# K and Q split two heads at a time, and put in place by DMA

## The chip, the cores and the metric

One core of a Trainium2 chip runs the whole program as one launch. The metric is device time in microseconds. A core has TensorE (PE in the profile; its weight loads are PEld), VectorE (DVE), ScalarE (ACT), GpSimd (POOL) and SyncE (SP), which here only issues DMAs. Each engine works through its own instructions in the order in which they were written; semaphores order the engines among each other.

## The reference

Inputs q, k, v are (2, 8, 576, 64): batch B, heads H, positions S, head width D. The output of an attention goes through two mixture-of-experts layers:

```python
scores = scale * np.matmul(q, k.transpose(0, 1, 3, 2))        # scale = 1/8
x = (np.log1p(np.abs(rel)) / psi_i)[..., None]                # rel = i - j
bias = np.maximum(x @ w1 + b1, 0.0) @ w2                      # (S, S, H)
scores = scores + bias.transpose(2, 0, 1)[None]
attn = softmax(scores)                                        # max taken off, then exp
x = (attn @ v), heads side by side: (1152, 512)
# layer 1: logits = normalised x @ normalised expert_emb / tau; layer 2: logits = x @ w_gate
# each: best expert per token, out = gate * relu(x @ w1[e]) @ w2[e]
```

All in float32, 8 experts, w1[e] (512, 1024), w2[e] (1024, 512).

## The kernel before

A float32 value is carried as two fp32r parts, a high one (a cast) and a low one (the rest), so that products keep their accuracy. **Attention** runs over 9 tiles `t` of 128 query rows; tiles 0, 2, 4, 6 belong to batch 0, tiles 1, 3, 5, 7 to batch 1, and tile 8 takes the last 64 rows of both. A tile has 8 heads: 72 steps (`heads`). For a step, `s_mm` (L317) multiplies Q by K on PE (4 matmuls, twice 288 columns, with the two parts of Q as weights), `s_max` (L325, DVE) adds the bias and finds the maximum, `s_exp` (L335, ACT) takes the exponent, `p_turn` (L349) transposes on PE, `p_out` (L359, L362, ACT) and `p_lo` (L368, DVE) copy out, and `av` (L388) multiplies by V on PE. `s_mm` and `s_max` of a step are written three steps ahead (`LEAD`), `s_exp` one.

**K** is resident: `K[p, head, j]` holds, for each of 16 (batch, head) pairs, the high part of all 64 dimensions in partitions 0 to 63 and the low part in partitions 64 to 127. So that both halves can be made in place, k is loaded twice, into both halves of `kraw` (L160). `k_split` (L162) casts all 128 partitions on ACT (L165) and overwrites the lower part on DVE (L166), for 2 heads at a time (`KCH`), 8 times in all. **Q** of a tile is `Q[p, part, head, i]` with the same 64 dimensions in both halves of the partitions; it is loaded twice (L143) and split on ACT (L151) and DVE (L152; for tile 0 on POOL).

**The bias** of 128 query rows is built in 18 pieces (`pc`) of 32 keys: `bias_mask` (L247, DVE), `bias_mm` (L260, 16 matmuls on PE), and `bias_out`, which either goes by ACT (L272) and POOL (L273, L274) or, where it is `direct`, by two DVE instructions (L268, L269). The first 18 pieces are made ahead of the first step (here called the preparation, together with splitting V); the pieces of later rows are spread over the steps by the table `sched`. `DIRECT` lists the direct pieces of the preparation. `KSLOT` says behind which step which K chunk is split, beside chunks 0 and 1 in the preparation.

`moe_setup2` (L637) prepares the router of the first layer: `g.en`, the scaled embeddings of the experts, and `g.wg`, the split gate weights of the second. The **experts** (from some 235 us on) then stream 64 weight chunks for each layer.

What is written in this order is handed to a scheduler, which orders the instructions of each engine by its own estimates; the order on an engine is therefore not that of the code, and moves when any part of the code does. Each DMA signals one of 8 semaphores in turn, and a DMA waits until the one 8 places ahead of it has landed.

Of the kernel before, what the change touches and what calls it, by code (L numbers as in the profile page):

```python
# [54 lines left out]
def layouts(inp):  # L55

    q, k, v = inp["q"], inp["k"], inp["v"]
    w1, b1, w2 = inp["w1"], inp["b1"], inp["w2"]
    qt = q.transpose(0, 3, 1, 2)
    vb = v.reshape(BH // 2, 2, S, D)  # L60
    vm = np.stack([vb[:, 0, 0:512], vb[:, 1, 64:576]], 1).reshape(BH, 4, P, D)
    vr = np.concatenate([vb[:, 0, 512:576], vb[:, 1, 0:64]], 1)
    wv = np.concatenate([w1.reshape(-1), b1.reshape(-1), w2.reshape(-1)])
    wc = np.concatenate([w1.reshape(HID, 1), b1.reshape(HID, 1), w2], 1)
    return {
        "a_q": np.stack([qt[:, :, :, i * P:(i + 1) * P] for i in range(4)]).reshape(4, B, D, H * P),
        "a_qt": qt[:, :, :, 512:576].reshape(B, D, H * 64),
        "a_k": k.transpose(0, 3, 1, 2).reshape(B, D, H * S),
        "a_v": vm.reshape(BH // 2, 2, 4, P, D).transpose(3, 1, 0, 2, 4).reshape(P, BH * 4 * D),
        "a_vr": vr.transpose(1, 0, 2).reshape(P, BH // 2 * D),  # L70
        "a_wv": wv.reshape(1, 320),
        "a_wc": np.concatenate([wc] * 4, 0),
    }
# [20 lines left out]
def attention(tc, ctx, g, a, out, setup, on_tile, on_slot):  # L94
# [38 lines left out]
    def q_load(t):  # L133
        o = tiles[t] = Ctx()
        o.e, o.av, o.Pt, o.pt, o.ps, o.qs = {}, {}, {}, {}, {}, []
        o.it = t // 2
        for b in ([t % 2] if t < 8 else [0, 1]):
            qr = soon.tile([P, H, P], F32, tag="qraw", name="qraw")
            if t == 8:
                nc.gpsimd.memset(qr, 0.0)  # L140
            for d in range(2):
                if t < 8:
                    nc.sync.dma_start(qr[d * 64:(d + 1) * 64].rearrange("p h i -> p (h i)"), a["a_q"][o.it, b])  # L143
                else:
                    nc.sync.dma_start(qr[d * 64:(d + 1) * 64, :, b * 64:b * 64 + 64], a["a_qt"][b].rearrange("d (h i) -> d h i", h=H))
            o.qs.append((b, qr, bw.tile([P, 2, H, P], F32R, tag="Q", name="Q", bufs=3)))
        o.sums = bw.tile([P, H], F32, tag="sums", name="sums")

    def q_split(t):
        for b, qr, Q in tiles[t].qs:  # L150
            nc.scalar.copy(Q[:, 0], qr)  # L151
            (nc.vector if t else nc.gpsimd).tensor_tensor(Q[:, 1], qr, Q[:, 0].bitcast(F32), ALU.subtract)  # L152

    kraws = {}

    def k_load(c):
        b, c4 = divmod(c, H // KCH)
        kr = kraws[c] = kp.tile([P, KCH * S], F32, tag="kraw", name="kraw")
        for d in range(2):
            nc.sync.dma_start(kr[d * 64:(d + 1) * 64], a["a_k"][b][:, c4 * KCH * S:(c4 + 1) * KCH * S])  # L160
# [12 lines left out]
    nc.vector.memset(zero, 0.0)
# [460 lines left out]
def moe_setup2(tc, g, a, pool, psum_tile):  # L634
    nc = tc.nc
    c = g.const
    g.trih = c.tile([P, P], F16, name="trih")  # L637
    nc.vector.tensor_copy(g.trih, g.tri)
    g.onesh = c.tile([P, P], F16, name="onesh")
    nc.vector.memset(g.onesh, 1.0)  # L640
    g.ioh = c.tile([P, P], F16, name="ioh")
    nc.vector.tensor_copy(g.ioh, g.iota)
    g.cap = c.tile([P, 1], F32, name="cap")
    nc.vector.tensor_copy(g.cap, g.cap64[:, 0:1])
    g.capp = c.tile([P, 1], F32, name="capp")
# [631 lines left out]
```

## Time and profile before

| | us |
|---|---|
| median of 3 runs | 635.23 (634.74 to 635.35) |
| the profiled execution | 635.61 |
| its span, first to last instruction | 633.7 |
| PE / DVE / ACT / POOL busy | 559.8 / 449.0 / 379.0 / 241.5 |
[...]

The span is read by stages: a share of busy time over the whole of it mixes the preparation, the steps of attention and the experts, and each has another engine that is full.

### The profile page before, as it was taken

How to read it: one execution, taken by the hardware profiler on the slowest of the kernel's cores; microseconds unless marked ns; L12 is line 12 of the kernel's file. 1: busy time of each engine (PE TensorE's matmuls, PEld its weight loads, DVE VectorE, ACT ScalarE, POOL GpSimd, SP SyncE). 2: the span in 40 equal slices, each digit the busy share in tenths (PEclk: the TensorE clock that was granted, in tenths of full speed). 3: DMA queues.
4: the chain of work that ended last, by engine and by line, in shares of the span. 5: the costliest groups of instructions: out<-in, count | busy, mean ns of one | idle time of the engine just before them, and what ended most of it. 6: DMA issues, size and time to landing. Idle time of an engine off the chain costs nothing. (4 is left out here: it accounts for less than half of the span.)

```text
span 633.7 us, 12729 instructions
## 1 busy us (share of the span) xinstructions
PE 559.8 (88%) x4770; PEld 477.5 (75%) x4770; DVE 449.0 (71%) x738; ACT 379.0 (60%) x629; POOL 241.5 (38%) x223
## 2 busy tenths in 40 slices
PE   2558889999999999799999999999879999899991
PEld 2447788998889997577788788777657887677771
DVE  6988999989987766889921541389668716738960
ACT  3347768877778755488723632587517536647840
POOL 3662643555545152324531312133232313424440
PEclk9568999999999999899999999999999999999996
DMA  7933651211000862789950451286938905847900
GB/s 215 324 90 79 166 179 36 69 53 43 19 19 26 206 234 84 241 272 342 359 169 25 137 186 49 76 279 213 348 89 234 350 35 169 271 145 228 327 5 8
DMA packets 48820, 101.42 MB, mean 160 GB/s; under 512 B 12820, under 2 KB 14740, under 8 KB 48448
## 3 DMA queue, kind: packets, MB, share of 16 engines
q1 hardware_dynamic: 41552, 92.12, 45.4%
q0 software_dynamic: 6272, 7.49, 3.6%
q8 instruction: 62, 1.02, 0.7%
q14 instruction: 54, 0.44, 0.2%
q10 hardware_dynamic: 880, 0.35, 0.2%
HBM read 97.47 MB, written 13.67 MB: 175 GB/s over the span
## 5 line engine op out<-in xcount | busy, mean ns | idle before, releaser
L911 DVE TENSOR_TENSOR wl<-raw,wh 128x1024 fp32r<-128x1024 f32 x125 | 156.2, 1289 | 19.5 <-ACT wh L898 15.9
L964 PE MATMUL py<-wh,hT 128*128 128x512 f32 x400 | 141.2, 404 | 0.0
L898 ACT CAST wh<-raw 128x1024 fp32r<-128x1024 f32 x110 | 113.9, 1050 | 5.1 <-ACTq L1169 2.6
L994 DVE TENSOR_TENSOR hT<-pt,hT 128x512 fp32r<-128x512 f32 x50 | 34.6, 692 | 92.4 <-ACT hT L993 92.4
L964 PEld LDWEIGHTS py<-wh,hT 128*128 128x128 f32 x400 | 75.2, 188 | 15.1
L260 PE MATMUL pm<-wmov,mask 128*128 128x64 f16 x1296 | 58.0, 203 | 29.6 <-DVE wmov L235 12.3
L273 POOL TENSOR_TENSOR btmp<-abst,xp 128x256 f32<-128x256 f32 x52 | 47.9, 920 | 84.0 <-ACT abst L272 81.9
L260 PEld LDWEIGHTS <-mask 128*128 128x128 f16 x1296 | 52.0, 105 | 36.3 <-DVE mask L247 25.3
L964 PE MATMUL py<-wl,hT 128*128 128x512 f32 x200 | 78.2, 391 | 0.0
L317 PE MATMUL s<-K,Q 128*128 128x288 f32 x320 | 64.0, 322 | 6.1 <-DVE mx L325 4.8
L335 ACT ACTIVATE P<-sb,mx 128x576 f32<-128x576 f32 x72 | 55.8, 776 | 17.5 <-DVE mx L325 15.4
L325 DVE CUSTOM_DVE_ANT_0 sb<-s,bias 128x576 f32<-128x576 f32 x72 | 53.4, 747 | 15.9 <-PE s L317 9.1
L247 DVE TENSOR_TENSOR mask<-toep,T 128x1024 f16<-128x1024 f16 x72 | 56.6, 792 | 1.5 <-PE pm L260 1.2
L964 PE MATMUL ph<-wh,xh 128*128 128x512 f32 x120 | 50.6, 421 | 7.8 <-PEq L1169 7.0
L349 PE MATMUL pt<-ident,P 128*128 128x128 f32 x324 | 53.1, 283 | 1.5 <-ACT pT L359 0.9
L317 PEld LDWEIGHTS s<-K,Q 128*128 128x128 f32 x320 | 46.9, 194 | 7.6 <-DVE mx L325 5.7
L272 ACT ACTIVATE abst<-pm,swi 128x512 f32<-128x512 f32 x52 | 35.7, 686 | 28.2 <-PE pm L260 28.0
L274 POOL TENSOR_TENSOR bias<-abst,btmp 128x256 f32<-128x256 f32 x52 | 50.0, 962 | 4.1
L993 ACT CAST hT<-pt 128x512 fp32r<-128x512 f32 x50 | 29.4, 587 | 36.4 <-PE pt L988 32.9
L964 PE MATMUL ph<-wh,xl 128*128 128x512 f32 x120 | 47.8, 398 | 1.4 <-issue 1.4
L964 PE MATMUL ph<-wl,xh 128*128 128x512 f32 x120 | 47.5, 396 | 0.0
L1033 POOL DMA_INDIRECT y_tok<-y,si x13 | 17.1, 1313 | 69.0 <-ACT y L1025 42.4
(218 smaller groups left out, 1144.9 us busy)
## 6 DMA issues: line engine op xcount, KB each, us to landing
raw<-m_w_dram SPq DMA_DIRECT2D x64, 512.0 KB, 5.2
raw<-n_w_dram SPq DMA_DIRECT2D x64, 512.0 KB, 5.1
kraw<-a_k_dram SPq DMA_DIRECT2D x16, 288.0 KB, 4.3
qraw<-a_q_dram SPq DMA_DIRECT2D x16, 256.0 KB, 4.2
out_dram<-zero SPq DMA_DIRECT2D x9, 256.0 KB, 7.3
y_tok<-zero SPq DMA_DIRECT2D x9, 256.0 KB, 4.8
x_tok<-x SPq DMA_DIRECT2D x8, 256.0 KB, 2.2
yt<-y_tok SPq DMA_DIRECT2D x4, 512.0 KB, 4.6
```

The costliest lines, as they stand in the source:

```text
L247: nc.vector.tensor_tensor(m, w, T[:, i0:i0 + P].unsqueeze(1).to_broadcast([P, 8, P]), ALU.is_gt)
L260: nc.tensor.matmul(pm[:, :, :, gq * 4:gq * 4 + 4], m[:, gq], wmov[:, part], start=part == 0, stop=part == 1)
L272: nc.scalar.mul(ab_, pm, isw)
L273: nc.gpsimd.tensor_tensor(tmp, ab_[:, 0], xp, ALU.mult)
L274: nc.gpsimd.tensor_tensor(biases[it][:, :, cs], ab_[:, 1], tmp, ALU.add)
L317: nc.tensor.matmul(ps[:, half, :288], Q[:, part, h], K[:, b * H + h, half * 288:half * 288 + 288], start=i == 0, stop=i == last)
L325: nc.vector.tensor_tensor_reduce(sb.rearrange("p (t j) -> p t j", t=2), o.ps.pop(h)[:, :, :288], biases[o.it][:, h].rearrange("p (t j) -> ...
L335: nc.scalar.activation(o.Pt[hp][:, x * S:(x + 1) * S], sb, AF.Exp, bias=mx, scale=-1.0, accum_out=o.sums[:, h:h + 1])
L349: nc.tensor.transpose(pt[:, cc], src, ident)
L898: eng.copy(hi, r)
L911: eng.tensor_tensor(lo, self.raw.pop((ge, j)), hi.bitcast(F32), ALU.subtract)
L964: self.nc.tensor.matmul(ps, x[a_][:, xs], w[b_][:, ws], start=first and i == 0, stop=last and i == 2)
```

## The change

K and Q are loaded once, with two heads above each other: head 2c in partitions 0 to 63, head 2c+1 in partitions 64 to 127. The split makes the high and the low part side by side in a scratch tile (`ks`, `qs`, one buffer each), and four DMAs from SBUF to SBUF put the parts where the matmuls want them. `Q` becomes `Q[p, head % 2, part, head // 2, i]`. The split of tile 8's Q and its POOL memset work on half the columns too. Of the preparation's bias pieces, 17 (the last) is direct in place of 15. K chunks 1 and 2 are written into the preparation's steps 8 and 14, the others two steps earlier than before. Two instructions of `moe_setup2` go from DVE to ACT.

```diff
-DIRECT = 1, 3, 5, 7, 9, 11, 13, 15
+DIRECT = 1, 3, 5, 7, 9, 11, 13, 17
-KSLOT = {0: 2, 2: 3, 4: 4, 6: 5, 8: 6, 10: 7}
+KSLOT = {0: 3, 2: 4, 4: 5, 6: 6, 8: 7}
...
-            for d in range(2):
-                if t < 8:
-                    nc.sync.dma_start(qr[d * 64:(d + 1) * 64].rearrange("p h i -> p (h i)"), a["a_q"][o.it, b])
...
+                nc.sync.dma_start(qr.rearrange("p h i -> p (h i)"), a["a_q"][o.it, b])
...
     def q_split(t):
         for b, qr, Q in tiles[t].qs:
-            nc.scalar.copy(Q[:, 0], qr)
-            (nc.vector if t else nc.gpsimd).tensor_tensor(Q[:, 1], qr, Q[:, 0].bitcast(F32), ALU.subtract)
+            qs = soon.tile([P, 2, H // 2, P], F32R, tag="qs", name="qs", bufs=1)
+            nc.scalar.copy(qs[:, 0], qr)
+            (nc.vector if t else nc.gpsimd).tensor_tensor(qs[:, 1], qr, qs[:, 0].bitcast(F32), ALU.subtract)
+            for half in range(2):
+                for par in range(2):
+                    nc.sync.dma_start(Q[half * 64:half * 64 + 64, par].bitcast(F32), qs[par * 64:par * 64 + 64].bitcast(F32))
...
     def k_split(c, eng):
         kr = kraws.pop(c)
-        dst = K[:, c * KCH:(c + 1) * KCH].rearrange("p h j -> p (h j)")
-        nc.scalar.copy(dst, kr)
-        eng.tensor_tensor(dst[64:], kr[64:], dst[64:].bitcast(F32), ALU.subtract)
-        if c + 2 < BH // KCH:
+        ks = soon.tile([P, 2, S], F32R, tag="ks", name="ks", bufs=1)
+        nc.scalar.copy(ks[:, 0], kr)
+        eng.tensor_tensor(ks[:, 1], kr, ks[:, 0].bitcast(F32), ALU.subtract)
+        for par in range(2):
+            for part in range(2):
+                nc.sync.dma_start(K[part * 64:part * 64 + 64, 2 * c + par].bitcast(F32), ks[par * 64:par * 64 + 64, part].bitcast(F32))
+        if c + 2 < BH // 2:
             k_load(c + 2)
...
-        if x == 12:
-            k_split(1, nc.vector)
+        if x in (8, 14):
+            k_split(x // 6, nc.vector)
...
-    nc.vector.tensor_scalar(g.en, g.en, ss, None, ALU.mult)
+    nc.scalar.mul(g.en, g.en, ss)
...
-    nc.vector.tensor_copy(g.wg[:, :, 0], g.wgr)
+    nc.scalar.copy(g.wg[:, :, 0], g.wgr)
```

Line numbers of the changed kernel are 1 to 5 higher (its K low part is L170, its Q low part L154, its copies L157 and L173, a mask L252, `s_max` L330).

On DVE, in the preparation behind the first mask of the bias (`mask`), before:

```order
L247 TENSOR_TENSOR mask<-toep,T 128x1024 x3
L654 TENSOR_SCALAR ess<-ess 8x1
L663 CAST wg<-wgr 128x4x8
L655 RECIPROCAL ess<-ess 8x1
L664 TENSOR_TENSOR wg<-wgr,wg 128x4x8
L656 TENSOR_SCALAR en<-en,ess 8x512
L268 SCALAR_TENSOR_TENSOR btmp<-pm,swi,xp 128x256
L247 TENSOR_TENSOR mask<-toep,T 128x1024
L166 TENSOR_TENSOR K<-kraw,K 64x1152
```

and at the same place of the changed kernel:

```order
L252 TENSOR_TENSOR mask<-toep,T 128x1024 x2
L170 TENSOR_TENSOR ks<-kraw,ks 128x576
L252 TENSOR_TENSOR mask<-toep,T 128x1024
L273 SCALAR_TENSOR_TENSOR btmp<-pm,swi,xp 128x256
L252 TENSOR_TENSOR mask<-toep,T 128x1024
```

The cast and the scaling have left DVE, and the small instructions of the router stand some 40 rows further down.

On DVE at the first four `s_max` (the rows named ISA), before; of the masks, 20 stand ahead of the first `s_max`, and both K chunks 0 and 1:

```order
L661 COPY enT<-pt 128x32
L247 TENSOR_TENSOR mask<-toep,T 128x1024
L325 ISA sb,mx<-s,bias 128x576
L325 ISA mx 128x1
L325 ISA sb,mx<-s,bias 128x576
L325 ISA mx 128x1
L247 TENSOR_TENSOR mask<-toep,T 128x1024
L325 ISA sb,mx<-s,bias 128x576
L325 ISA mx 128x1
L325 ISA sb,mx<-s,bias 128x576
```

and now, where 22 masks, K chunk 0 and the Q of tile 1 stand ahead of it, and K chunk 1 (`ks`) behind the first:

```order
L252 TENSOR_TENSOR mask<-toep,T 128x1024 x2
L154 TENSOR_TENSOR qs<-qraw,qs 128x512
L330 ISA sb,mx<-s,bias 128x576
L330 ISA mx 128x1
L252 TENSOR_TENSOR mask<-toep,T 128x1024
L170 TENSOR_TENSOR ks<-kraw,ks 128x576
L330 ISA sb,mx<-s,bias 128x576
L330 ISA mx 128x1
L273 SCALAR_TENSOR_TENSOR btmp<-pm,swi,xp 128x256
L274 SCALAR_TENSOR_TENSOR bias<-pm,swi,btmp 128x8x32
L252 TENSOR_TENSOR mask<-toep,T 128x1024
L373 SCALAR_TENSOR_TENSOR ptl<-pt,pth 128x512
```

The third `s_max` follows directly; it is the first that needs K chunk 1. On both sides, chunk c (from 2 on) is split one or no step ahead of its first use.

On SP, from the nine writes of zeros into the output on, the queue now reads:

```order
L200 DMA out_dram<-zero 128x512 x9
L157 DMA Q<-qs 64x1024 x4
L173 DMA K<-ks 64x576 x4
L163 DMA kraw<-a_k_dram 128x576
L130 DMA xp<-c_xpos_dram 128x576
L157 DMA Q<-qs 64x1024
L173 DMA K<-ks 64x576 x4
L163 DMA kraw<-a_k_dram 128x576
L157 DMA Q<-qs 64x1024
L173 DMA K<-ks 64x576 x4
```

Before, only loads and writes of zeros stood there; now 72 copies are in this queue (8 K chunks and 10 splits of Q, 4 each), and a matmul waits for each of them.

## Rows read from the trace of the kernel before

**Rows 1.** The page: busy time, share of the span and instructions of each engine.

```profile
PE 559.8 (88%) x4770; PEld 477.5 (75%) x4770; DVE 449.0 (71%) x738; ACT 379.0 (60%) x629; POOL 241.5 (38%) x223
```

**Rows 2.** By stretch: length; busy PE, PEld, DVE, ACT, POOL; clock, DMA, GB/s.

```profile
12.00:41.00 29.00, 16.52 (x266) 14.82 (x267) 27.94 (x56) 13.87 (x20) 18.51 (x17) 0.62 0.82 247
41.00:48.00 7.00, 4.16 (x61) 3.78 (x58) 3.99 (x8) 2.06 (x3) 6.61 (x7) 0.88 0.33 91
48.00:60.00 12.00, 9.76 (x95) 9.12 (x95) 10.58 (x21) 9.22 (x19) 1.38 (x2) 0.86 0.23 54
60.00:100.00 40.00, 33.78 (x510) 30.44 (x507) 38.24 (x69) 31.40 (x58) 22.81 (x24) 1.00 0.57 160
100.00:140.00 40.00, 39.74 (x594) 38.14 (x593) 37.91 (x80) 31.79 (x66) 18.51 (x22) 1.00 0.20 55
140.00:200.00 60.00, 55.49 (x834) 51.83 (x832) 54.44 (x112) 45.49 (x96) 34.45 (x38) 1.00 0.09 26
200.00:235.00 35.00, 35.00 (x395) 34.12 (x392) 23.57 (x58) 26.02 (x59) 13.22 (x9) 1.00 0.67 197
```

**Rows 3.** In order of time, DVE, ACT and POOL, 8 to 23 us: start, duration.

```profile
8.96 0.22 DVE L642 CAST ioh<-cm 128x128 f16<-128x128 f32 x1
...
12.40 1.90 DVE L247 TENSOR_TENSOR mask<-toep,T 128x1024 f16<-128x1024 f16 x3
...
14.68 1.15 ACT L165 CAST K<-kraw 128x1152 fp32r<-128x1152 f32 x1 [0.45 <-DMA kraw<-a_k_dram]
14.73 2.34 POOL L152 TENSOR_TENSOR Q<-qraw,Q 128x1024 fp32r<-128x1024 f32 x1
...
14.84 2.96 DVE L663 CAST wg<-wgr 128x32 fp32r<-128x32 f32 x1
...
17.95 0.94 DVE L656 TENSOR_SCALAR en<-en,ess 8x512 f32<-8x512 f32 x1
...
20.32 1.77 DVE L166 TENSOR_TENSOR K<-kraw,K 64x1152 fp32r<-64x1152 f32 x1
```

**Rows 4.** In order of time, DVE, up to the first `s_max`.

```profile
44.25 0.73 DVE L247 TENSOR_TENSOR mask<-toep,T 128x1024 f16<-128x1024 f16 x1
48.00 0.76 DVE L325 CUSTOM_DVE_ANT_0 sb<-s,bias 128x576 f32<-128x576 f32 x1 [3.01 <-POOL bias L274]
```

**Rows 5.** The low parts of K and Q by line: shortest, median, longest ns.

```profile
L166 DVE TENSOR_TENSOR K<-kraw,K x8: 1354/1355/1768, 20.3 to 87.1; 64x1152 fp32r<-64x1152 f32 x8
L152 DVE TENSOR_TENSOR Q<-qraw,Q x9: 1212/1221/1747, 56.0 to 206.1; 128x1024 fp32r<-128x1024 f32 x9
```

**Rows 6.** DVE by line: busy us, mean ns; and one `s_mm` on PE.

```profile
L247 DVE TENSOR_TENSOR mask<-toep,T 128x1024 f16<-128x1024 f16 x72 | 56.6, 792 | 1.5 <-PE pm L260 1.2
...
L368 DVE SCALAR_TENSOR_TENSOR ptl<-pt,pth 128x512 f16<-128x512 f32 x36 | 24.5, 679 | 4.7 <-ACT pth L362 4.5
...
L268 DVE SCALAR_TENSOR_TENSOR btmp<-pm,swi,xp 128x256 f32<-128x256 f32 x29 | 13.7, 473 | 2.5 <-PE pm L260 2.0 <-POOL bias L274 0.4
...
216.72 0.78 PE L317 MATMUL s<-K,Q 128*128 128x288 f32 x4
```

**Rows 7.** DMA issues: count, KB, us to landing; and L276, the first `bias<-bias`.

```profile
bias<-bias SPq DMA_DIRECT2D x3, 576.0 KB, 5.8
...
x_tok<-x SPq DMA_DIRECT2D x2, 128.0 KB, 2.3
...
DMA to landing us min/median/max: 4.6/4.6/4.6
```

**Rows 8.** SP's queue in order of time: start, time to issue.

```profile
18.26 8.53 SPq L195 DMA_DIRECT2D out_dram<-zero  x9
...
67.03 1.10 SPq L160 DMA_DIRECT2D kraw<-a_k_dram  x2
...
211.96 0.59 SPq L278 DMA_DIRECT2D bias<-bias  x1
213.59 0.32 SPq L679 DMA_DIRECT2D x_tok<-x  x1
```

More of the change, by code (lines that the diff above doesn't have):

```diff
@@ L28 @@
 EXPM = 0x7F800000
-KCH = 2
 PSC = 4096.0
-DIRECT = 1, 3, 5, 7, 9, 11, 13, 15
+DIRECT = 1, 3, 5, 7, 9, 11, 13, 17
 XSTEP = 1, 2, 3, 4
 WA = 0, 0, 4
-KSLOT = {0: 2, 2: 3, 4: 4, 6: 5, 8: 6, 10: 7}
+KSLOT = {0: 3, 2: 4, 4: 5, 6: 6, 8: 7}
 def consts():
@@ L58, in layouts, with pairs @@
     w1, b1, w2 = inp["w1"], inp["b1"], inp["w2"]
-    qt = q.transpose(0, 3, 1, 2)
+    def pairs(x):
+        return x.reshape(B, H // 2, 2, S, D).transpose(0, 2, 4, 1, 3).reshape(B, P, H // 2, S)
+    qt = pairs(q)
     vb = v.reshape(BH // 2, 2, S, D)
@@ L65, in layouts @@
     return {
-        "a_q": np.stack([qt[:, :, :, i * P:(i + 1) * P] for i in range(4)]).reshape(4, B, D, H * P),
-        "a_qt": qt[:, :, :, 512:576].reshape(B, D, H * 64),
-        "a_k": k.transpose(0, 3, 1, 2).reshape(B, D, H * S),
+        "a_q": np.stack([qt[:, :, :, i * P:(i + 1) * P] for i in range(4)]).reshape(4, B, P, H // 2 * P),
+        "a_qt": qt[:, :, :, 512:576].reshape(B, P, H // 2 * 64),
+        "a_k": pairs(k).transpose(0, 2, 1, 3),
         "a_v": vm.reshape(BH // 2, 2, 4, P, D).transpose(3, 1, 0, 2, 4).reshape(P, BH * 4 * D),
@@ L137, in q_load @@
         for b in ([t % 2] if t < 8 else [0, 1]):
-            qr = soon.tile([P, H, P], F32, tag="qraw", name="qraw")
+            qr = soon.tile([P, H // 2, P], F32, tag="qraw", name="qraw")
             if t == 8:
                 nc.gpsimd.memset(qr, 0.0)
-            for d in range(2):
-                if t < 8:
-                    nc.sync.dma_start(qr[d * 64:(d + 1) * 64].rearrange("p h i -> p (h i)"), a["a_q"][o.it, b])
-                else:
-                    nc.sync.dma_start(qr[d * 64:(d + 1) * 64, :, b * 64:b * 64 + 64], a["a_qt"][b].rearrange("d (h i) -> d h i", h=H))
-            o.qs.append((b, qr, bw.tile([P, 2, H, P], F32R, tag="Q", name="Q", bufs=3)))
+                nc.sync.dma_start(qr[:, :, b * 64:b * 64 + 64], a["a_qt"][b].rearrange("p (h i) -> p h i", h=H // 2))
+            else:
+                nc.sync.dma_start(qr.rearrange("p h i -> p (h i)"), a["a_q"][o.it, b])
+            o.qs.append((b, qr, bw.tile([P, 2, 2, H // 2, P], F32R, tag="Q", name="Q", bufs=3)))
         o.sums = bw.tile([P, H], F32, tag="sums", name="sums")
@@ L150, in q_split @@
         for b, qr, Q in tiles[t].qs:
-            nc.scalar.copy(Q[:, 0], qr)
-            (nc.vector if t else nc.gpsimd).tensor_tensor(Q[:, 1], qr, Q[:, 0].bitcast(F32), ALU.subtract)
+            qs = soon.tile([P, 2, H // 2, P], F32R, tag="qs", name="qs", bufs=1)
[4 more added lines that the diff above has]
+                    nc.sync.dma_start(Q[half * 64:half * 64 + 64, par].bitcast(F32), qs[par * 64:par * 64 + 64].bitcast(F32))
     kraws = {}
     def k_load(c):
[L157 to L160, printed above, removed]
+        kr = kraws[c] = soon.tile([P, S], F32, tag="kraw", name="kraw")
+        nc.sync.dma_start(kr, a["a_k"][c // 4, c % 4])
     def k_split(c, eng):
         kr = kraws.pop(c)
-        dst = K[:, c * KCH:(c + 1) * KCH].rearrange("p h j -> p (h j)")
-        nc.scalar.copy(dst, kr)
-        eng.tensor_tensor(dst[64:], kr[64:], dst[64:].bitcast(F32), ALU.subtract)
-        if c + 2 < BH // KCH:
+        ks = soon.tile([P, 2, S], F32R, tag="ks", name="ks", bufs=1)
[5 more added lines that the diff above has]
+        if c + 2 < BH // 2:
             k_load(c + 2)
-    kp = soon
     zero = soon.tile([P, DM], F32, name="zero", bufs=1)
@@ L316, in s_mm @@
                 for part in range(2):
-                    nc.tensor.matmul(ps[:, half, :288], Q[:, part, h], K[:, b * H + h, half * 288:half * 288 + 288],
+                    nc.tensor.matmul(ps[:, half, :288], Q[:, h % 2, part, h // 2], K[:, b * H + h, half * 288:half * 288 + 288],
                                      start=i == 0, stop=i == last)
```

## The prediction

> **What bounds the kernel now.** The page comes first, and it misleads: PE is busy for 88% and DVE for 71% of the span [rows 1], as if DVE hardly mattered. The table of stretches shows where that is wrong [rows 2]. From 12 to 41 us DVE is busy for 27.94 of 29 us and PE for 16.52: the preparation is DVE's. From 48 to 100 us DVE is busy for 48.8 of 52 us, PE for 43.5. From 100 to 140 both are nearly full (PE 39.74 of 40, DVE 37.91), to 200 neither quite, and from 200 to 235 PE has no gap at all. So an instruction taken off DVE is worth its length before 100 us, little from 100 to 200, and nothing from 200 to 235. The experts behind are not touched, and start when attention is done: what is won ahead of 235 us shifts them as a whole.
>
> In order of time the preparation shows what fills DVE [rows 3]: a cast of 128x32 that lasts 2.96 us, where another cast with four times the columns took 0.22; it begins just after POOL's pass over Q (14.73 to 17.07) and ends with it. Then 0.94 us for an 8x512 scaling, and 1.77 for K chunk 0. Further on, before the first `s_max` at 48.00, stands a wait of 3.01 us for POOL's last bias piece [rows 4].
>
> **The change, part by part.**
>
> *Low parts of K and Q.* DVE's time follows the columns: 1152 take 1.355 us and 1024 take 1.221 [rows 5]. Half the columns: 0.68 and 0.61 us, by those rates. ACT's casts halve too, but ACT has room (31.4 of 40 us [rows 2]), so they count nothing, as do the cast and the scaling that go to it. Loads halve. Only the first matters: DVE now comes to chunk 0 behind its third mask, at some 13.7 us, and ACT's cast of it waited for the load until 14.68 [rows 3]. With one load of Q ahead of it instead of two, and half the bytes, it should land by 13: 0 to 1.5 us, I take 0.
>
> *The preparation,* from the first `s_max` at 48.00 backwards. Off DVE: the wait 3.0 (piece 17 goes to DVE, POOL's last is now 16, and the order puts two masks and a Q split in the place of the wait), the cast 2.9, the scaling 0.9, of chunk 0 1.77 - 0.68 = 1.1, and chunk 1, which moves behind the first `s_max`, 1.4 [rows 5]: 9.3 us. On DVE: two masks that stood later, 1.4 at 0.7 each [rows 4], tile 1's Q split, 0.6, and POOL's Q pass, which with half the columns should take 1.2 us instead of 2.34, and now lies beside DVE's second and third mask. What that costs is open: nothing, as three masks ran at 0.63 us each (1.90 for three [rows 3]) beside POOL's instruction ahead of the pass, or 1.2, as the cast waited for the whole pass. I take 0.8, nearer the cast, since it is the same POOL instruction. Added 2.8, net 6.5: first `s_max` at 41.5.
>
> [...]
>
> The state at that `s_max` is not the old one: two masks (1.4) and a Q split (1.2 at its old length) are done, chunk 1 (0.68) is not. That is another 1.9 us that DVE needn't spend later.
>
> *48 to 100 us.* Chunks 2 to 7 save 6 x 0.68 = 4.1, tile 2's Q 0.6. DVE thus offers 6.5 + 1.9 + 4.7 = 13.1 us by the old 100 us mark.
>
> *The copies* take some of it back. For K the chain is: low part on DVE, SP issues the copy, it lands, `s_mm` (0.78 [rows 6]), `s_max`. No copy of 144 KB between 64 partitions is in the trace. The nearest row is 64 rows of x to HBM, 128 KB, 2.3 us to landing; the far end is the 576 KB copy of the bias inside SBUF, 4.6 us, as many bytes as all four K copies together [rows 7]. With 0.1 for the signal the need is 3.2 to 5.5 us. The second low copy is issued 0.55 later (two loads take 1.10 [rows 8]), so I take 3.5, near the row of like size.
>
> What covers it is what stands on DVE between the low part and the first `s_max` that needs the chunk, at 0.79 a mask, 0.47 a direct half, 0.68 a `p_lo`, 0.75 an `s_max` [rows 4, 6]: for chunks 1 to 7 3.2, 3.2, 4.0, 4.5, 3.8, 4.1 and, with two masks and a `p_lo` alone, 2.3 us. At a need of 3.5 DVE waits 0.3 + 0.3 + 1.2 = 1.8 us, at 3.2 some 0.9, at 5.5 some 13. K chunk 0 and tile 0's Q come behind the nine writes of zeros, which were issued by 26.8 us [rows 8]; eight copies at 0.55 and some 3 us to land bring them to 34, 6 us ahead of the first `s_mm`. Q splits of later tiles stand at least 4 steps, some 10 us, ahead of use, against 4 copies of 0.55 and some 3 us to land: nothing. Without that cover each would cost up to 5.
>
> [...]
>
> So DVE leaves 13.1 - 1.8 = 11.3. PE sets another limit: from 41 to 100 it is busy for 47.7 us [rows 2]. In the new order PE starts `s_mm` some 1.5 us ahead of the first `s_max`, at 40, with 2.2 us of later bias matmuls already done: 45.5 us of work. If it idles as from 60 to 100 us (15.5%), the mark falls at 40 + 53.8 = 93.8, 6.2 us early; if as from 100 to 140 (0.7%), 14 us early. With DVE's load lighter it lies between; I take the middle of 6.2 and 11.3: **8.8 us**.
>
> *100 to 235 us.* Seven Q splits save 4.3 us of DVE; PE has 4.8 us of idle time there, all before 200 [rows 2]. I take 1.0 of a possible 0 to 4.3. Against it, SP's order now puts the store of x ahead of the third copy of the bias of tile 8, which used to go first, 1.6 us apart, with two Q copies behind [rows 8]: 0 to 1.9 us on tile 8's first step, of which I take 0.5.
>
> **Sum:** 8.8 + 1.0 - 0.5 = 9.3 us off the profiled 635.61 is 626.3. The median of the runs lies 0.38 lower: **625.9**.
>
> **Rivals.**
> - *The copies land as late as the bias copy* (need 4.6 to 5.5): DVE waits 7 to 13 us at the K chunks, and the gain is 0 to 6. For it speaks that all four are in flight together; against it the 2.3 us of the x rows. Some 631.
> - *Slower:* the same place, but each K copy sits behind others in SP's queue. A Q copy of 256 KB stands directly ahead of six of the seven K groups from chunk 1 on. From a need of some 5.5 us on, the waits eat everything that DVE saves; at 6.5 they come to 20 us, and the time is 642. Against it: the Q copies there depend on splits that DVE has finished earlier.
> - *POOL stays the last:* pieces 14, 15, 16 now follow each other on it. If the first `s_max` waits for it as before, up to 2 us less: 628.
> - *PE is the bound after all,* with its old idle share: 6.2 - 1.8 + 0.5, 631. Or it follows DVE fully and the tiles to 200 us gain too: 620.
>
> **Chances.** The forecast with its spread, POOL included, 0.70; fuller gain, 0.08; late copies or PE's old share, gain still above 1.3 us (0.2%, about what a measurement of this kernel can tell), 0.10; nothing left, 0.05; slower by more than 0.2%, 0.07. Faster 0.88, same 0.05, slower 0.07. The range reaches from the fuller gain, 620, to the late copies, 632; it leaves out the far end of both.
>
> **What would show it.** [...] The prediction is wrong if `s_mm` waits for a K copy by over 2 us at every chunk, if POOL or the queue of SP holds the first `s_max`, or if PE's idle share to 100 us stays at 15%.

## The result, and the profile after

The change makes the kernel slower: 640.76 us median (639.07 to 642.45) against 635.29, ratio 1.0086, 95% interval 1.0062 to 1.0109. Measured a second time (run e8 below) it is 639.69 us, ratio 1.0029 [1.0000, 1.0058]. The loss is thus 0.3 to 0.9%, the smaller figure at the edge of what its interval tells, where a gain of 1.5% was forecast. The profiled execution took 639.07 us, with a span of 637.3.

The page of the changed kernel, busy times and instructions, answers to [rows 1]: DVE has 9.6 us less to do.

```profile
PE 564.9 (89%) x4770; PEld 481.2 (76%) x4770; DVE 439.4 (69%) x736; ACT 371.5 (58%) x631; POOL 237.0 (37%) x223
```

The stretches, with the columns of [rows 2]:

```profile
12.00:41.00 29.00, 17.09 (x300) 14.84 (x301) 26.96 (x59) 12.14 (x19) 21.23 (x20) 0.76 0.76 233
41.00:48.00 7.00, 4.44 (x42) 3.86 (x39) 7.00 (x12) 3.01 (x6) 4.25 (x5) 0.53 0.13 27
48.00:60.00 12.00, 10.23 (x90) 8.90 (x90) 6.24 (x14) 5.79 (x12) 2.92 (x4) 0.56 0.53 125
60.00:100.00 40.00, 34.70 (x485) 31.05 (x484) 33.78 (x66) 26.55 (x55) 16.56 (x18) 1.00 0.76 186
140.00:200.00 60.00, 58.75 (x899) 55.88 (x898) 55.29 (x117) 47.95 (x102) 32.87 (x38) 1.00 0.30 75
200.00:235.00 35.00, 32.27 (x345) 30.92 (x343) 23.30 (x52) 22.06 (x52) 13.21 (x9) 1.00 0.70 194
```

Two stretches stand out. From 48 to 60 us DVE works 6.24 us instead of 10.58, and PE's granted clock is 0.56 instead of 0.86: it stays at a lower level of 0.50 from 48 to 58 us. From 200 to 235, where PE had no gap, it has 2.7 us of them.

The 72 `s_max` follow each other in the order of the steps, and serve as milestones (start in us; "gap 8" is from the last `s_max` of tile 7, head 63, to the first of tile 8; "end" is the span's end minus the last `s_max`). Beside them stand all runs of the experiments. Each ratio is to the kernel before as it was measured beside that run (medians of 635.29 to 637.01 us), so medians of runs that were measured at different times are not to be subtracted from each other. The milestones are of one execution each; those of e2, e5, e7, e8 and e9 took 2.1 to 4.9 us more than the median of their kernel.

| run | median, ratio [95%] | first | third | head 63 | gap 8 | last | end |
|---|---|---|---|---|---|---|---|
| before | 635.29 | 48.00 | 49.97 | 217.57 | 3.31 | 237.23 | 396.5 |
| after | 640.76, 1.0086 [1.0062, 1.0109] | 45.95 | 55.57 | 215.79 | 6.79 | 238.99 | 398.3 |
| e1 | 635.95, 1.0006 [0.9986, 1.0027] | 47.48 | 49.65 | 217.37 | 3.31 | 237.03 | 396.0 |
| e2 | 638.85, 1.0036 [1.0014, 1.0058] | 46.66 | 48.83 | 215.85 | 6.78 | 239.64 | 399.5 |
| e3 | 640.95, 1.0069 [1.0042, 1.0096] | 45.79 | 47.98 | 214.47 | 6.79 | 237.50 | 402.1 |
| e4 | 640.33, 1.0020 [0.9985, 1.0055] | 45.28 | 53.82 | 218.16 | 6.62 | 241.69 | 397.2 |
| e5 | 638.79, 1.0023 [0.9996, 1.0049] | 45.30 | 54.93 | 220.76 | 3.31 | 240.43 | 401.5 |
| e6 | 632.79, 0.9938 [0.9914, 0.9963] | 46.27 | 48.47 | 212.43 | 3.31 | 232.10 | 397.6 |
| e7 | 639.40, 1.0024 [0.9996, 1.0053] | 43.83 | 52.12 | 215.71 | 6.78 | 239.08 | 401.5 |
| e8 | 639.69, 1.0029 [1.0000, 1.0058] | 45.82 | 55.44 | 219.29 | 6.78 | 242.69 | 398.5 |
| e9 | 632.54, 0.9929 [0.9903, 0.9955] | 46.06 | 47.73 | 213.81 | 3.31 | 233.47 | 399.4 |
| e10 | 631.01, 0.9922 [0.9894, 0.9949] | 46.34 | 48.50 | 212.83 | 3.31 | 232.51 | 395.9 |
| e11 | 639.71, 1.0055 [1.0033, 1.0077] | 49.18 | 51.35 | 220.66 | 3.31 | 240.34 | 398.8 |
| e12 | 636.84, 1.0017 [0.9993, 1.0041] | 44.13 | 52.44 | 212.08 | 6.78 | 235.22 | 400.0 |
| e13 | 635.50, 0.9988 [0.9965, 1.0010] | 46.03 | 48.20 | 217.28 | 3.31 | 237.03 | 396.6 |
| e14 | 677.19, 1.0643 [1.0605, 1.0680] | 50.62 | 52.75 | 243.60 | 18.12 | 279.39 | 396.0 |

So the profiled loss of 3.6 us of span is made up of 1.8 us won up to head 63, 3.5 lost at tile 8, and 1.8 in the experts; and the first `s_max` gained 2.05 us where 6.5 were forecast, the third lost 5.6.

Four places in the changed kernel show this. First the preparation, DVE and POOL in order of time (to be held against [rows 3]):

```profile
11.01 1.26 POOL L154 TENSOR_TENSOR qs<-qraw,qs 128x512 fp32r<-128x512 f32 x1 [8.65 <-ACT qs L153]
11.05 1.53 DVE L229 TENSOR_SCALAR T<-tt,sc 128x576 f16<-128x576 f32 x1
...
13.55 3.19 POOL L658 TENSOR_TENSOR ess<-ess,half 8x1 f32<-8x1 f32 x1 [1.28 <-ACT esq L657]
...
16.61 1.40 DVE L252 TENSOR_TENSOR mask<-toep,T 128x1024 f16<-128x1024 f16 x1
16.73 0.72 POOL L278 TENSOR_TENSOR btmp<-abst,xp 128x256 f32<-128x256 f32 x1
...
22.84 0.48 DVE L273 SCALAR_TENSOR_TENSOR btmp<-pm,swi,xp 128x256 f32<-128x256 f32 x1 [1.41 <-POOL bias L279]
```

POOL's pass over Q is there, 1.26 us (1.2 forecast), and the DVE instruction beside it lasts 1.53 us (0.52 where POOL is idle, run e7). Then the first steps, DVE:

```profile
45.95 0.74 DVE L330 CUSTOM_DVE_ANT_0 sb<-s,bias 128x576 f32<-128x576 f32 x1
...
47.24 0.74 DVE L170 TENSOR_TENSOR ks<-kraw,ks 128x576 fp32r<-128x576 f32 x1
47.90 0.74 DVE L330 CUSTOM_DVE_ANT_0 sb<-s,bias 128x576 f32<-128x576 f32 x1
...
53.34 0.70 DVE L252 TENSOR_TENSOR mask<-toep,T 128x1024 f16<-128x1024 f16 x1 [3.77 <-PE pm L265]
53.96 0.68 DVE L373 SCALAR_TENSOR_TENSOR ptl<-pt,pth 128x512 f16<-128x512 f32 x1
55.57 0.76 DVE L330 CUSTOM_DVE_ANT_0 sb<-s,bias 128x576 f32<-128x576 f32 x1 [0.94 <-PE s L322]
```

DVE waits for PE, and PE meanwhile runs what the order puts ahead of the third `s_mm` (transposes, `av`, bias pieces), at the lower clock:

```profile
47.81 1.08 PE L354 MATMUL pt<-ident,P 128*128 128x128 f32 x4 [1.90 <-ACT P L340]
49.57 1.97 PE L393 MATMUL acc<-V,pT 128*128 128x64 f32 x8 [0.68 <-ACT pT L364]
...
54.24 1.30 PE L322 MATMUL s<-K,Q 128*128 128x288 f32 x4
```

Before, the third `s_mm` stood ahead of the first transpose:

```profile
48.82 0.82 PE L317 MATMUL s<-K,Q 128*128 128x288 f32 x4 [2.80 <-DVE mx L325]
...
50.13 1.05 PE L349 MATMUL pt<-ident,P 128*128 128x128 f32 x4
```

The lower clock is the smaller part of it: in e4, where it holds there only from 48.6 to 52.0 us, the third `s_max` still comes 6.6 us behind the second (7.7 in the changed kernel).

Tile 8, SP's queue, where the two Q copies stand behind the third bias copy:

```profile
211.82 0.32 SPq L684 DMA_DIRECT2D x_tok<-x  x1
212.25 0.60 SPq L283 DMA_DIRECT2D bias<-bias  x1
212.90 2.80 SPq L157 DMA_DIRECT2D Q<-qs  x2
```

PE, however, isn't seen to wait for them. From 216.0 to 222.6 us it is busy throughout (stretch, with the columns of [rows 2]), and the first matmuls of `s_mm` of tile 8, of which 8 follow each other before, stand apart, with transposes and `av` of other heads between them:

```profile
216.00:222.60 6.60, 6.60 (x82) 6.52 (x80) 2.68 (x9) 3.23 (x8) 1.03 (x1) 1.00 0.94 276
...
217.66 0.51 PE L322 MATMUL s<-K,Q 128*128 128x288 f32 x2
...
218.76 0.51 PE L322 MATMUL s<-K,Q 128*128 128x288 f32 x2
...
221.41 1.04 PE L322 MATMUL s<-K,Q 128*128 128x288 f32 x6
```

and before:

```profile
219.43 1.31 PE L317 MATMUL s<-K,Q 128*128 128x288 f32 x8
```

So here too it is the order on PE that the copies changed. Behind it PE has two gaps, 1.8 and 0.8 us, until DVE is done, which works on rows of the router that last longer than in e5 below (1.67 us in place of 0.22):

```profile
223.51 1.67 DVE L744 TENSOR_TENSOR d<-lg,mx 128x56 f32<-128x56 f32 x1
```

And all that PE waits for a K copy from 48 to 110 us, from the view of who waited for whom (us in total, times, longest):

```profile
PE s L322 <- DMA K<-ks: 0.2, 1, 0.2
```

### The profile page after: what moved, and what is told of

The parts are those of the page before. It is cut to its first block, busy times and chain, and to the rows that moved or that the text cites. A ratio compares the mean times of both kernels' runs of the same rounds, so it can differ in the third digit from the quotient of the medians.

```text
span 637.3 us, 12851 instructions
## 1 busy us (share of the span) xinstructions
PE 564.9 (89%) x4770; PEld 481.2 (76%) x4770; DVE 439.4 (69%) x736; ACT 371.5 (58%) x631; POOL 237.0 (37%) x223
## 5 line engine op out<-in xcount | busy, mean ns | idle before, releaser
L916 DVE TENSOR_TENSOR wl<-raw,wh 128x1024 fp32r<-128x1024 f32 x125 | 153.7, 1268 | 22.0 <-ACT wh L903 16.6
L278 POOL TENSOR_TENSOR btmp<-abst,xp 128x256 f32<-128x256 f32 x52 | 44.9, 864 | 88.2 <-ACT abst L277 79.2
L330 DVE CUSTOM_DVE_ANT_0 sb<-s,bias 128x576 f32<-128x576 f32 x72 | 53.6, 749 | 16.1 <-PE s L322 14.5
L252 DVE TENSOR_TENSOR mask<-toep,T 128x1024 f16<-128x1024 f16 x72 | 58.7, 819 | 6.5 <-PE pm L265 6.1
L279 POOL TENSOR_TENSOR bias<-abst,btmp 128x256 f32<-128x256 f32 x52 | 47.9, 921 | 4.1
L969 PEld LDWEIGHTS py<-wl,hT 128*128 128x128 f32 x200 | 37.8, 189 | 6.5
```

The costliest lines, as they stand in the source:

```text
L252: nc.vector.tensor_tensor(m, w, T[:, i0:i0 + P].unsqueeze(1).to_broadcast([P, 8, P]), ALU.is_gt)
L278: nc.gpsimd.tensor_tensor(tmp, ab_[:, 0], xp, ALU.mult)
L279: nc.gpsimd.tensor_tensor(biases[it][:, :, cs], ab_[:, 1], tmp, ALU.add)
L330: nc.vector.tensor_tensor_reduce(sb.rearrange("p (t j) -> p t j", t=2), o.ps.pop(h)[:, :, :288], biases[o.it][:, h].rearrange("p (t j) -> ...
L916: eng.tensor_tensor(lo, self.raw.pop((ge, j)), hi.bitcast(F32), ALU.subtract)
L969: self.nc.tensor.matmul(ps, x[a_][:, xs], w[b_][:, ws], start=first and i == 0, stop=last and i == 2)
```

## The experiments

The theory after the result: the gain goes at two places, the lost lead at the third step and tile 8 (first taken for the queue of SP), and DVE's time in the preparation is partly POOL's. The rivals: copies that hold back every chunk; the ACT moves and the direct piece themselves; a mere shift of the clock.

**e1, the two ACT moves and the direct piece alone, on the kernel before.**

```diff
-DIRECT = 1, 3, 5, 7, 9, 11, 13, 15
+DIRECT = 1, 3, 5, 7, 9, 11, 13, 17
...
-    nc.vector.tensor_scalar(g.en, g.en, ss, None, ALU.mult)
+    nc.scalar.mul(g.en, g.en, ss)
...
-    nc.vector.tensor_copy(g.wg[:, :, 0], g.wgr)
+    nc.scalar.copy(g.wg[:, :, 0], g.wgr)
```

> K and Q as in the kernel before; only the two instructions that go to ACT and the direct last bias piece. Lost lead (the loss of the change comes from K chunk 1, whose scratch buffer and copies come too late for the first steps): this part has no copies, the first s_max comes 2 to 5 us ahead of 48.00, and the time is 630 to 634. Copies everywhere (each chunk's copies hold the steps back): the same, 630 to 634. Engine moves (POOL and ACT are what holds the preparation, so the moves bring nothing or hurt): the first s_max at 47 to 48.5, the time 635 or more.

635.95 us, no change, first `s_max` at 47.48: the rival's numbers. In order of time, DVE and POOL:

```profile
14.60 2.33 POOL L152 TENSOR_TENSOR Q<-qraw,Q 128x1024 fp32r<-128x1024 f32 x1
...
14.71 2.95 DVE L664 TENSOR_TENSOR wg<-wgr,wg 128x32 fp32r<-128x32 f32 x1
16.90 0.71 POOL L273 TENSOR_TENSOR btmp<-abst,xp 128x256 f32<-128x256 f32 x1
```

The cast has left DVE, and the next instruction, a subtraction of 128x32, takes its 2.95 us, to the end of POOL's second instruction. The time was never the cast's.

**e12, the other half: K and Q by copies alone** (the changed kernel with those three edits undone).

> K and Q by copies alone, without the ACT moves and with the last piece on POOL as before. Lost lead and tile 8 are in this part: the third s_max comes 6 us or more behind the second, tile 8's first 6.6 to 6.8 us behind head 63, head 71 at 238.5 to 241, median 638 to 642. If the ACT moves and the direct piece have a share in the loss: 635 to 637.

636.84 us, within the interval no change, the number of the second case, by which the ACT moves and the direct piece have a share in the loss. Against the second measurement of the changed kernel (1.0029 [1.0000, 1.0058]) the time alone doesn't show it, since the intervals overlap. Gap 8 is 6.78, as said; the third `s_max` is 5.2 us behind the second, less than said, and head 71 comes at 235.22, not 238.5 or later. The first comes at 44.13, earlier than with the ACT moves. The cast on DVE, here far from POOL's pass over Q, and beside a POOL instruction (38.30 to 39.47 us) that ends with it, so that its own length is at most this:

```profile
39.26 0.24 DVE L668 CAST wg<-wgr 128x32 fp32r<-128x32 f32 x1
```

So the moves to ACT save at most 0.24 and some 0.5 us there, not 3.8, and in the changed kernel they, with the direct piece, go with a later start by 1.8 us.

**e2, Q by copies, K as before** (K's lines of the diff undone).

> The changed kernel with K as before (loaded twice, split in place, no copies), Q still by copies. Lost lead: the third s_max follows the second within 2 us as before, the 6 us at that place are gone, the 3.5 us at tile 8 stay: 633 to 636. Copies everywhere, and those of Q as much as those of K: half of the loss or more stays, 637 to 640. Engine moves: no better than the changed kernel, 639 to 641.

638.85 us. Heads 2 and 3 follow at once and head 63 is 1.7 us early, but gap 8 is 6.78 and the experts take 399.5 us: the gain of the lead is not seen in the time, which is the number of the rival (copies everywhere). The trace doesn't bear the rival out: no K copy is left, and what is lost against before stands at tile 8 and in the experts.

**e3, chunk 1 early.** Its scratch tile gets memory that lives only in the preparation, so it needn't wait for chunk 0's copies.

```diff
-        ks = soon.tile([P, 2, S], F32R, tag="ks", name="ks", bufs=1)
+        ks = (prep if c == 1 else soon).tile([P, 2, S], F32R, tag="ks", name="ks", bufs=1)
```

> The changed kernel, but the scratch tile of K chunk 1 has memory of its own, so its split needn't wait until chunk 0's copies have landed; all copies stay. Lost lead: chunk 1 is split some 20 us ahead of the first s_max, the third s_max follows the second within 2 us, and the time is 633 to 636. Copies everywhere: the wait moves to chunks 2 and 3, 638 to 641. Engine moves: 639 to 641.

The third `s_max` comes at 47.98, 7.6 us earlier than in the changed kernel, at once behind the second: the place is right. The time is 640.95, the rivals' number: the lead alone doesn't set it. Head 63 is 3.1 us ahead of before, gap 8 takes 3.5 of them, and the experts 5.6.

**e4 and e5, tile 8.** e4 loads tile 8's raw Q into both halves and splits it in place, so no copy stands in the queue; e5 also lets POOL's first pass over the experts' weights wait for the router's choice on DVE, and has POOL's first three passes written behind steps 3, 4 and 5 in place of 1, 3 and 5.

```diff
+            if t == 8:
+                nc.scalar.copy(Q[:, :, 0], qr)
+                nc.vector.tensor_tensor(Q[:, :, 1], qr, Q[:, :, 0].bitcast(F32), ALU.subtract)
+                continue
...
-        if step % 2 == 1 and step // 2 < NE:
-            self.hi(0, step // 2, G)
-            self.lo(0, step // 2, G)
+        if step in (3, 4, 5):
+            self.hi(0, step - 3, G)
+            self.lo(0, step - 3, G)
...
+            if k == 3:
+                tiny = ex[1].T("tiny", [1])
+                ex[0].nc.gpsimd.tensor_scalar(tiny, ex[1].oh[:, 0, 0:1], 1.0, 0.0, ALU.mult, ALU.add)
```

> The changed kernel, but tile 8's two Q parts are loaded into both halves and split in place, without copies, so that nothing but the x rows stands between the bias copies in SP's queue. If the queue at tile 8 costs the 3.5 us that are lost there (tail): the first s_max of tile 8 comes some 3 us earlier against head 63 than in the changed kernel, and the time is 636 to 638. If what is seen there is only the state of the clock or of PE: 640 to 641. Lost lead alone says nothing against either, and expects the 6 us at the third s_max to stay.

> As the run with tile 8 split in place, but POOL's first pass over the experts' weights waits until the router's choice is made on DVE (a POOL instruction of one column reads it first). Collision (small DVE instructions of the router are held by POOL's passes of 1.05 and 2.4 us): they take 0.2 us each as in the kernel before, tile 8's first s_max comes 3.3 to 3.6 us behind that of head 63 (3.31 before, 6.8 in all kernels with the copies), head 71 follows head 63 by 19.7 to 20.5 us in place of 23.2, and the time is 636 to 638 without further clock dips. Queue (the third bias copy or the raw loads are late): the 6.6 to 6.8 us stay, 640 to 641.

Without the copies the gap stays at 6.62, but for another reason. e4, DVE and POOL:

```profile
219.95 1.05 POOL L915 TENSOR_SCALAR wh<-raw 128x1024 fp32r<-128x1024 f32 x1 [3.12 <-DMA raw<-m_w_dram]
...
220.33 0.73 DVE L754 TENSOR_TENSOR d<-lg,mx 128x56 f32<-128x56 f32 x1
221.09 2.38 POOL L926 TENSOR_TENSOR wl<-raw,wh 128x1024 fp32r<-128x1024 f32 x1
221.10 2.44 DVE L755 SCALAR_TENSOR_TENSOR ev<-d,cm 128x56 f32<-128x56 f32 x1
...
224.56 2.35 POOL L926 TENSOR_TENSOR wl<-raw,wh 128x1024 fp32r<-128x1024 f32 x1
224.78 0.76 DVE L340 CUSTOM_DVE_ANT_0 sb<-s,bias 128x576 f32<-128x576 f32 x1
```

and e5:

```profile
222.93 0.22 DVE L754 TENSOR_TENSOR d<-lg,mx 128x56 f32<-128x56 f32 x1
223.18 0.22 DVE L755 SCALAR_TENSOR_TENSOR ev<-d,cm 128x56 f32<-128x56 f32 x1
...
224.07 0.76 DVE L340 CUSTOM_DVE_ANT_0 sb<-s,bias 128x576 f32<-128x576 f32 x1
224.14 1.05 POOL L915 TENSOR_SCALAR wh<-raw 128x1024 fp32r<-128x1024 f32 x1
```

An instruction over 128x56 that takes 0.22 us lasts 2.44 beside POOL's, and ends with it (at 223.54 and 223.47 us). With POOL behind the choice the gap is 3.31, that of before; the time, 638.79, falls short of what was expected; why isn't shown (its profile, of an execution of 643.64 us, has the clock at its lower level from 99.0 to 105.8 us and at three places in the experts). So two things made tile 8 late: the order on PE that comes with the Q copies (no Q copies and no help in e11: 3.31), and POOL's passes that meet the router once the order around it shifts. e4's runs spread over 14 us (633.25 to 647.06); its median says little.

**e6, all three mends**, and **e9**, with tile 0's Q low part on DVE as well (the edit of e7).

> The changed kernel with chunk 1 early, tile 8 in place, and POOL behind the router's choice. If the lost lead and the collision are the two places where the gain went: head 63 near 214.5, head 71 near 234.3 (3 us ahead of before), the time 631.5 to 634. If the experts take it back (dips of the granted clock behind 240 us, 1.7 us each as the six profiles so far have it): the attention ends early as said, and the time is 635 to 639.

> The three mends together (chunk 1 early, tile 8 in place, POOL behind the router's choice) and tile 0's Q low part on DVE. Hold adds up: the first s_max comes 2 us earlier than with the three alone (46.27), at some 44.2, and head 63 at 210.5 to 212; time 630.5 to 632.5. PE is full behind 100 us and takes it back: head 63 within 0.7 us of the 212.43 that the three alone have; time 632 to 634.

e6: 632.79 us, faster than both kernels. Head 63 at 212.43, gap 3.31, last `s_max` at 232.10, 5.1 us ahead of before. e3 and e5 hardly moved the time alone; together the mends give 7 us over the changed kernel (639.69, e8, measured beside it). Why they give more together isn't shown. e9 adds nothing: 632.54 us, its first `s_max` at 46.06, not 44.2, and its head 63 at 213.81, which neither case said.

**e7, tile 0's Q low part on DVE, nothing else.**

```diff
-            (nc.vector if t else nc.gpsimd).tensor_tensor(qs[:, 1], qr, qs[:, 0].bitcast(F32), ALU.subtract)
+            nc.vector.tensor_tensor(qs[:, 1], qr, qs[:, 0].bitcast(F32), ALU.subtract)
```

> The changed kernel, but tile 0's Q low part is made by DVE (0.6 us), not by POOL (1.26 us). Held by POOL (a DVE instruction that starts beside POOL's pass lasts until it ends): the scaling of T takes 0.51 us in place of 1.53, so that DVE loses no more than it did, the first s_max comes at 45.0 to 46.0 (45.95), and the time changes by under 1 us. Own cost (durations on DVE are its own): 0.6 more on DVE, first s_max at 46.5 or later. Neither expects the attention's end to move by more than 1 us.

More work on DVE, and the first `s_max` comes 2.1 us earlier, at 43.83, earlier than either case said. Of this, 1.0 is `T`, 0.9 the masks, and 1.1 tile 1's Q split, which the new order puts behind it; the new instruction costs 0.6. DVE in order of time:

```profile
11.00 0.52 DVE L229 TENSOR_SCALAR T<-tt,sc 128x576 f16<-128x576 f32 x1
...
11.50 0.69 DVE L154 TENSOR_TENSOR qs<-qraw,qs 128x512 fp32r<-128x512 f32 x1
```

The time is the changed kernel's: head 4 is 3.7 us earlier, head 63 0.1.

**e10, the kernel before with e1's edits and tile 0's Q low part on DVE; no copies.**

> The kernel before with the two ACT moves, the direct last piece, and tile 0's Q low part on DVE (1.2 us) in place of POOL (2.3 us); no copies at all. Held by POOL: no DVE instruction of the first 20 us lasts 2.9 us any more (the cast before, the subtraction of wg with the ACT moves alone), and the first s_max comes at 45 to 46.5 in place of 47.48; the time is 633.5 to 635.5. Own cost: 1.2 us more on DVE, the first s_max at 48 or later, 636 or more.

631.01 us, ratio 0.9922, the lowest median of all, and better than expected, with the first `s_max` at 46.34 and head 63 4.7 us ahead of before. The copies are not needed for what e6 gains. That the whole of it comes from the hold is not shown: see e13.

**e11, chunk 1 early, Q as before.**

> The changed kernel with chunk 1 early and Q as before (loaded twice, split in place), K by copies. If the Q copies are what makes tile 8 late: its first s_max comes 3.3 us behind head 63 without any help, head 71 19.7 us behind; third s_max within 2 us of the second; time 632.5 to 635. If the bias copy or the raw loads are the cause: 6.6 to 6.8 us at tile 8, 637 to 640.

Gap 8 is 3.31 without help, so the Q copies, by the order that comes with them, are the first cause there. All else is worse than expected: first `s_max` at 49.18, 639.71 us. POOL's pass over Q has its old length again, and beside it now stands K chunk 0 (0.74 us long in e12):

```profile
14.05 4.15 DVE L168 TENSOR_TENSOR ks<-kraw,ks 128x576 fp32r<-128x576 f32 x1
```

**e8, the changed kernel again.**

> The changed kernel unchanged, to see what of its loss is the same in each execution. Two parts (attention longer by a fixed amount, the experts longer by the number of clock dips in them): head 64 again 6.8 us behind head 63 and head 71 at 238.5 to 239.5; from there to the end 394.8 us and 1.7 for each dip listed behind 240 us (396.5 with one in the profile of before, 398.3 with two in that of after); median 639 to 641. Attention alone: all runs within 1 us of each other.

Gap, median and the experts' length are as said; but the attention is not the same twice: head 71 comes at 242.69, later than said, and head 63 is 3.5 us later than in the first profile. The runs spread over 11 us, where attention alone would have kept them within 1. The hold differs as well: beside POOL's pass over Q stands not `T` (0.51 us here) but the cast behind it (1.23 us, 0.16 in the first profile). In e8 the granted clock is at its lower level from 98.5 to 105.3 us, which begins 1.2 us behind a wait of PE for a K copy (chunk 7):

```profile
97.33 1.53 PE L322 MATMUL s<-K,Q 128*128 128x288 f32 x8 [1.18 <-DMA K<-ks]
```

**e13 and e14, the experts.** In the three kernels without copies the last column of the table is 395.9 to 396.5, in the eleven profiles with copies on SP 397.2 to 402.1, although the order of the experts' instructions is the same. The lower clock is not all of it: between 240 and 600 us the profiles of before, e1, e10, e4, e6 and e12 have one such spell each, and the first three take 395.9 to 396.5 us, the others 397.2 to 400.0. PE's waits behind the last `s_max` that end with its own sequencer ("PEq") or with nothing that the profile shows ("issue") add up to 8.8 to 9.7 us in the three kernels without copies, and to 10.6 to 13.2 in the eleven. Two of them, in the second layer, here of after:

```profile
540.80 0.49 PE L969 MATMUL ph<-wh,xh 128*128 128x512 f32 x1 [2.12 <-PEq L1174]
545.52 0.40 PE L969 MATMUL ph<-wh,xl 128*128 128x512 f32 x1 [2.62 <-issue]
```

Before, they are 1.68 and 1.38. They are not at this place in all: e6 and e9 have one wait there, of 1.96 and 1.93 us, and two others some 100 us earlier. e13 adds to e10 as many DMAs of SP as the changed kernel has more, of 256 bytes each; e14 has ACT issue the 72 copies.

```diff
+            nc.sync.dma_start(dm[i:i + 1, :], g.ones[i:i + 1, 0:64])
```

```diff
-                    nc.sync.dma_start(Q[half * 64:half * 64 + 64, par].bitcast(F32), qs[par * 64:par * 64 + 64].bitcast(F32))
+                    nc.scalar.dma_start(Q[half * 64:half * 64 + 64, par].bitcast(F32), qs[par * 64:par * 64 + 64].bitcast(F32))
```

> The kernel of the last but two runs (before, with the ACT moves, the direct piece and tile 0's Q low part on DVE; no copies), plus 54 DMAs of 256 bytes from SP, three behind each split, which nothing waits for: as many DMAs as the changed kernel has more. If the number of DMAs in SP's program or queue is what makes the experts longer with the copies: the two waits of PE at the one branch of the second layer (near 304 us behind head 71: 1.4 and 1.8 us without copies, 2.1 and 2.6 with) come to 4 us or more together, head 71 to the end takes 397.5 to 400 us (395.9 without copies), median 632.5 to 634.5. If it is the copies themselves, or where the program's parts lie: 2.9 to 3.3 us, 395.5 to 397, median 630.5 to 632.

> The changed kernel with all 72 copies issued by ACT, not SP. For the start: SP is free, and the split of K chunk 1 comes ahead of the first s_max, so that the third s_max follows the second within 2 us; but each copy takes ACT 0.5 to 0.7 us and waits there for DVE's low part, so ACT is late at many steps. For the experts: if SP's program or queue makes them longer, head 71 to the end takes 395.5 to 397 us, and the two waits at the branch 2.9 to 3.3 us; if the copies do it whoever issues them, 398 or more, and 4 us or more. Time 636 to 645, as ACT's share of attention grows by 40 us of issuing.

e13: waits of 1.45 and 1.38 us, experts 396.6. So it isn't the number of DMAs. The time, 635.50, is later than either case said: with e10's edits and its early first `s_max` (46.03), head 63 is 4.5 us later; the order moved again. So e10's gain hangs on the order behind the start too. e14: 396.0 us for the experts, a single wait of 0.37 us at that place, less than either case said, and 40 us lost in attention, whose tile 8 waits 9 us for a Q copy (677.19 us, where 636 to 645 were expected). With attention ending so much later it is no clean comparison. The longer experts go with copies that SP issues; by what way, these runs don't show.

## Why the prediction was wrong, step by step

- **Preparation: "Off DVE ... the cast 2.9, the scaling 0.9".** This step failed. The 2.96 us [rows 3] were taken for time that leaves DVE with the cast, although the prediction saw POOL's pass beside it; they are POOL's. The cast doesn't end with that pass (17.07) either, but at 17.80, with POOL's next instruction (17.75). The hold passes on: to the subtraction of `wg` (e1, 2.95), to K chunk 0 (e11, 4.15), in the changed kernel to the scaling of `T` (1.53) and to the masks. Summed from each row's start to the next, up to the first `s_max`, some 7.8 us left DVE there (waits 2.0 in place of 3.0, `wg` 2.4, the scaling 0.9, K 2.5) where 9.3 were forecast, and 5.6 came where 2.8 were: masks 3.3 (two more, and 0.78 us each on average in place of 0.70), `T` 1.0, tile 1's Q split 1.1, V's split 0.2. With the small ones, net 2.05 us, not 6.5. Two rows of before, POOL's neighbours of the pass over Q:

```profile
12.31 2.42 POOL L653 TENSOR_TENSOR ess<-ess,half 8x1 f32<-8x1 f32 x1 [9.96 <-ACT esq L652]
...
17.04 0.71 POOL L273 TENSOR_TENSOR btmp<-abst,xp 128x256 f32<-128x256 f32 x1
```

Rows beside a POOL instruction, against the same row at another place: K chunk 0's low part 4.15 us (e11) against 0.74 (e12), the router's 128x56 row 2.44 (e4) against 0.22 (e5), the scaling of `T` 1.53 (after) against 0.52 (e7), the cast 2.96 (before) against at most 0.24 (e12). `s_max`, which reads the scores from PSUM, takes 0.76 us beside POOL's pass of 2.35 us (e4, from 224.56), and 0.74 at 47.90 in after, where POOL does nothing from 46 to 54 us. The prediction priced the hold at 0.8 us, on the masks alone; that it meets other rows of DVE too was missed. The masks of 0.63 us, from which it took that the hold might cost nothing, read as the same hold the other way round: it was POOL's instruction beside them that lasted, 2.42 us over 8x1 (0.69 in e10, where no mask stands beside it).
- **"Chunk 1, which moves behind the first s_max" was booked as a gain, with a cover of 3.2 us on DVE.** This failed too. The cover was counted on DVE alone. In PE's order the third `s_mm` then stands behind two transposes, an `av` and bias pieces, which before came after it. It cost 5.6 us against before at the third `s_max`; e3 gives 7.6 back.
- **The copies' need of 3.5 us per chunk, 1.8 us of waits, mostly at chunk 7.** Right or too high: PE waits 0.2 us for a K copy up to 110 us, in e8 1.18, at chunk 7 (and the weight load of the third `s_mm` 0.7 us for nothing that the profile names). The time to landing wasn't in the profile. The 0.1 us for the signal was the author's estimate, and no row of a copy shows it; the third `s_max` of after starts 0.03 us behind the end of the `s_mm` that it waits for, as the profile models that end. The rivals of late copies and a full queue at each chunk fall.
- **"8.8 us by the 100 us mark".** Over-sized even with the mends: head 16, near that mark, comes 3.9 us early in e6, 3.7 in e10; it is 2.7 late in after. The step took PE's idle share to fall below the 15.5% of before from 60 to 100 us, since DVE has less to do. It hardly did: it is 13.3% in after, and with the early starts of e6 and e10 15.1% and 13.2%. This was one of the prediction's own signs of being wrong, and its rival that keeps the old share was nearer to what came. Early starts shrink behind it, as PE is nearly full (38.86 of 40 us in after from 100 to 140): 3.7 us at head 4 are 0.1 at head 63 from after to e7; the late start of after shrinks in the same way.
- **Tile 8: 0.5 of 0 to 1.9.** The place was right, by luck, since the mechanism was not: SP's queue was priced, and what came was PE's order, with no wait for a copy to be seen, and POOL's passes beside the router, which weren't in the sum. It cost 3.5 us in every kernel with tile 8's Q by copies (more in e14, where PE does wait for them).
- **"What is won ahead shifts them as a whole".** Failed: the experts take 397 to 402 us with the copies on SP. Dips of the granted clock are a part of it (between 240 and 600 us one in the profile of before, near 266 us, two in that of after, near 449 and 549, all three down to about 0.50, and three in e3's, the last of double length), PE's longer waits another. Why those are longer stays open.
- **Low parts 0.68 and 0.61 us:** measured medians 0.75 and 0.68; DVE's total fell by 9.6 us. The work went as planned; the time did not follow it.

## What to carry to other kernels

A long row for a tiny instruction can be a wait that the profile doesn't name: look at what the other engine does in those microseconds, and price the edit by the same instruction away from that engine's long one (at most 0.24, not 2.96 us). When a split or a load moves behind the first use of something else, read the order on the engine that consumes it as well (at the third step and at tile 8 PE was late without waiting for a copy), not only what covers it on the engine that makes it. And mends that show nothing one by one (e3, e5) can be worth 1% together (e6), so measure milestones in the trace beside the total.

## What the runs showed of the hardware

- POOL's side of the hold: its `pow` over 8x1 takes 0.61 us or less in e3 and e12, and 3.19 us in the first profile of the changed kernel, beside DVE's masks and K chunk 0. In the second profile of the same kernel (e8) it takes 0.66: which engine is held can change from one execution to the next.
- The experts' part depends on something other than its own instructions: its length and PE's waits for its sequencer or for nothing shown (8.8 us in all before, 11.6 after) were greater in every profile with copies issued by SP, of which the last is issued at 213.6 us in after, ahead of the experts, and not with the same number of tiny DMAs (e13: 396.6 us, 9.9).
- SP's queue before: the nine writes of zeros read none of the loads, and yet eight of them wait, one for V (0.8 us), two for VR (1.0), two for K (1.9), two for Q (1.3) and one for the first write (0.2). In the queue these eight stand 8 places ahead of the second to the ninth write.
